# Two more groups per token pair with seven second products in layer 2, on paired operand sets

## The chip, the cores and the metric

One core of a Trainium2 chip runs the whole program. The metric is the device time of one execution in microseconds. An engine is TensorE (PE in the rows, PEld its weight loads), VectorE (DVE), ScalarE (ACT), GpSimd (POOL) or SyncE (SP).

## The reference

Attention over the channels (256) of 6016 tokens, then two feed-forward layers with 2048 hidden channels each. Only the second layer is changed:

```python
def _moe2_ref(x, w_in, w_out):      # x: 6016 x 256, w_in: 256 x 2048, w_out: 2048 x 256
    h = np.maximum(x @ w_in, 0.0)
    return (h * h @ w_out).astype(np.float32)
```

All of it is float32.

## The kernel before

Tokens are worked in six pairs of column blocks: five pairs of 2 x 512 tokens and one of 2 x 448. The hidden channels are worked in eight groups of 2 x 128. One pair and one group make a step; layer 1 takes steps 0 to 47, layer 2 steps 48 to 95. A 128 x 128 weight block times a block of tokens is a product. Both operands are split into a rounded high half and a low half, so a product is three matmuls: high by high, low by high, high by low. A split is a ScalarE copy (high half) and a VectorE subtraction (low half).

In a step the first products make a 2 x 2 block of hidden values (two rows of channels, two column blocks of tokens) out of a 2 x 2 block of weights and a 2 x 2 block of tokens. The Strassen-Winograd scheme does this with seven products in place of eight: p1 to p7, on sums of weights (made ahead) and sums of tokens (t1 to t4, made in `tokens`, line 770). The second products multiply the activated hidden block, 2 x 2, by a 2 x 2 block of output weights and add into PSUM over the eight groups. They are eight by the plain way and can be seven by the same scheme, if sums of hidden blocks are made in every step.

Layer 2's pairs 1 to 5 run through `first7s` (line 1583). Its PSUM banks X and Y hold the first products in turn. A bank is read out by ScalarE (`snap`) or added to by VectorE (`total`) before the next product may go on in it; Y also serves for those second products that have no bank of their own and are added to SBUF by VectorE (`flush`, line 1762). The four hidden blocks of a step lie in R[0] to R[3]: h11, h12, h21, h22. ReLU and square are two ScalarE operations (`relu`, `square`) or one VectorE operation (`both`).

`S2SET` (line 1459) names the groups with seven second products: 0, 2, 4, 6 of each pair, 0, 2, 4 of the last. For such a group three hidden blocks go straight into products (u[1], u[2], u[3], `items_direct`), and four sums (`tail`, line 1702) into four more (`items_sums`): t1 = R1 + R0 on VectorE, then t3 = R0 + R2, t2 = t1 + R2, t4 = R3 + t2 by three accumulating DMAs that GpSimd issues (`move`, line 1660). Each is split when it is made. The direct products stand in the next step, the four others three steps after the group's own. Other groups (plain) split all four blocks and have eight products in the next step (`items_plain`), two of which go through Y into `fz`. `finish_a` and `finish_b` (lines 1857, 1880) make the four output blocks of a pair in the first steps of the next, `finish_last` and `finish_rest` those of the last pair after all steps. `sums2` (line 1489) makes the sums of output weights for a group, once, ahead of pair 1.

The order of the work is computed ahead by the class `Plan` (line 28). TensorE and the DMA queue run in the order in which operations are added. For VectorE, ScalarE and GpSimd the planner simulates the engines with a fixed cost for each operation (`act_us`, `dve_us`, `MOVE_US`, `MOVE_LAT`) and issues each engine's operations by rank, which begins as the latest time at which each may start. `blame` looks for gaps of TensorE and lowers the rank of what they waited for; the best of 200 rounds is issued.

Of the kernel before, what the change touches and what calls it, by code (L numbers as in the profile page):

```python
# [18 lines left out]
P = 128  # L19
# [3 lines left out]
class Op:  # L23
    def __init__(self, eng, cost, lat, fn, deps):
        self.eng, self.cost, self.lat, self.fn, self.deps = eng, cost, lat, fn, deps


class Plan:
# [9 lines left out]
    ROUNDS = 200  # L38

    def __init__(self):  # L40
        self.ops = []
# [68 lines left out]
    def blame(self):  # L110

        for o in self.ops:
            if o.eng != "PE" or o.idle < 0.03:
                continue
            x = o
            while x.deps:
# [3 lines left out]
                x.rank -= 0.5 * min(1.0, o.idle + 0.2)  # L120

    def issue(self):
# [18 lines left out]
        for o in reversed(ops):  # L141
            for u in users[id(o)]:
                o.late = min(o.late, u.late - o.lat - o.cost)
            if o.eng == "DMA":

                o.late = queue = min(o.late, queue - o.cost)
        for o in ops:
            o.rank = o.late
        best = None
        for _ in range(self.ROUNDS):  # L150
# [3 lines left out]
            self.blame()  # L154
# [25 lines left out]
MOVE_US, MOVE_LAT = 0.9, 6.2  # L180
# [8 lines left out]
def tile_kernel(  # L189
# [50 lines left out]
    XS, GB, WB = 9, 4, 2  # L240
# [87 lines left out]
    def words(name, src, outs, lat=1.1):  # L328
# [3 lines left out]
        def f_e():  # L332
            t["e"] = cv_p.tile([P, 512], U32, tag="e", name="e")
            t["m"] = cv_p.tile([P, 512], U32, tag="m", name="m")
# [40 lines left out]
    def pair_of(name, src, place, *deps, lat=1.1):  # L375
# [5 lines left out]
        def f_e():  # L381
            t["e"] = cv_p.tile([P, 512], U32, tag="e", name="e")
            t["m"] = cv_p.tile([P, 512], U32, tag="m", name="m")
# [387 lines left out]
    def tokens(l, pr, parts=False):  # L771
# [28 lines left out]
        def tt(i):  # L800
            return t["t"][:, i, :n]

        def f_t3():
            t["t"] = xr_p.tile([P, 3, TB], F32, tag="t", name=f"xt{l}{pr}")
            V.tensor_tensor(tt(2), b(1, 1), b(0, 1), ALU.subtract)

        if plain(l, pr):
            todo = [(f"b{i + 1}{j + 1}", lambda i=i, j=j: b(i, j), load) for j in range(2) for i in range(2)]
            ts = []
        else:  # L810
            c = dve_us(n)
            sub = ALU.subtract
            t3 = ordered("xt", add("DVE", c, f_t3, load, xt_r.take()))
            t1 = add("DVE", c, lambda: V.tensor_tensor(tt(0), b(0, 1), b(0, 0), sub), t3)
            t2 = add("DVE", c, lambda: V.tensor_tensor(tt(1), b(1, 1), tt(0), sub), t1)
            t4 = add("DVE", c, lambda: V.tensor_tensor(b(0, 1), b(1, 0), tt(1), sub), t2)
            ts = [t1, t2, t3, t4]
            todo = [
# [1264 lines left out]
```

## Time and profile before

| what | before |
|---|---|
| device time, median of 3 runs | 1027.79 us (1026.01 to 1029.95) |
| the profiled execution | 1027.78 us |
| its span, first to last instruction | 1026.0 us |
| TensorE busy | 1019.3 us, 4565 matmuls |
| VectorE busy | 867.0 us, 1372 operations |
| ScalarE busy | 794.9 us, 1287 operations |
| GpSimd busy | 69.5 us, 78 operations |

Busy time is the union of an engine's instructions; consecutive ones overlap, so an instruction's printed length is more than its distance from the next. The first pair of layer 2 (plain second products) runs from about 550 to 628 us, pairs 1 to 4 from there to 941, the last to the end.

### The profile page before, as it was taken

To read this page: it belongs to the slowest core of one execution; us is meant where nothing else is said; L and a number is where in the kernel's file an instruction comes from. 1 tells how busy PE (TensorE), PEld (TensorE's weight loads), DVE (VectorE), ACT (ScalarE), POOL (GpSimd) and SP (SyncE) were. 2 spreads that over 40 slices of the span, in tenths; PEclk is the share of its full clock that TensorE was granted. 3 is DMA by queue.
4 is the path that set the end of the run, shared out by engine and by line. 5 is a ranking of instruction groups with operands and counts; after the bars stand their busy time and mean duration, and the time that the engine had idled before them with its cause. 6 is when DMAs were issued, how large, how long until landed. Compare 5 with 4: busy or idle time off the path is not lost.

```text
span 1026.0 us, 13020 instructions
## 1 busy us (share of the span) xinstructions
PE 1019.3 (99%) x4565; PEld 855.0 (83%) x4565; DVE 867.0 (85%) x1372; ACT 794.9 (77%) x1287; POOL 69.5 (7%) x78
## 2 busy tenths in 40 slices
PE   9999999999999999999999999999999999999998
PEld 7888888888888888888998888888888888888897
DVE  3999988888989899898778886788888888888876
ACT  5787667677778777768768978889889789789784
POOL 3400000000000000000000000111111111111110
PEclk9999999999999999999999999999999999999999
DMA  9657447435454644635745323655665665664661
GB/s 360 264 175 238 141 134 226 159 126 197 149 185 147 207 169 149 206 128 160 276 151 199 133 92 127 187 142 155 159 176 144 167 174 128 172 177 126 175 160 45
DMA packets 62609, 174.10 MB, mean 170 GB/s; under 512 B 6992, under 2 KB 10192, under 8 KB 61264
## 3 DMA queue, kind: packets, MB, share of 16 engines
q1 hardware_dynamic: 54336, 158.62, 46.0%
q0 software_dynamic: 8208, 14.65, 8.3%
q8 instruction: 36, 0.59, 0.2%
q14 instruction: 29, 0.24, 0.1%
HBM read 126.35 MB, written 32.24 MB: 155 GB/s over the span
## 4 chain that ended last, share of the span: by engine, by line
PE 97%; DMA 1%; DVE 0%; SPq 0%; ACT 0%; issue 0%
PE acc L1386 10%; PE acc L1392 10%; PE acc L1387 10%; PE xy L1602 6%; PE xy L1604 6%; PE xy L1603 6%; PE A L1293 4%; PE A L1294 4%; PE A L1295 4%; PE acc L1738 3%; PE acc L1740 3%; PE acc L1739 3%; PE s L925 3%; PE B L1295 2%; PE B L1293 2%; PE B L1294 2%
## 5 line engine op out<-in xcount | busy, mean ns | idle before, releaser
L1386 PE MATMUL acc<-g,wo 128*128 128x512 f32 (+1 forms) x448 | 172.9, 386 | 0.0
L1387 PE MATMUL acc<-g,wo 128*128 128x512 f32 (+1 forms) x448 | 172.9, 386 | 0.0
L1179 DVE TENSOR_TENSOR g<-r,g 128x1024 fp32r<-128x1024 f32 (+1 forms) x112 | 135.0, 1206 | 23.9 <-ACT g L1175 23.7
L1175 ACT ACTIVATE g<-r 128x1024 fp32r<-128x1024 f32 (+1 forms) x112 | 117.1, 1046 | 46.2 <-DVE r L1149 45.5
L1392 PE MATMUL acc<-g,wo 128*128 128x512 f32 (+1 forms) x448 | 136.6, 386 | 0.0
L1662 POOL DMA_DIRECT2D rs<-rs x57 | 49.3, 865 | 912.4 <-ACT rp L1633 601.5
L1652 DVE TENSOR_TENSOR gs<-rs,gs 128x512 fp32r<-128x512 f32 (+1 forms) x137 | 89.9, 674 | 14.6 <-ACT gs L1648 13.2
L1392 PEld LDWEIGHTS acc<-g,wo 128*128 128x128 f32 x448 | 84.1, 188 | 16.2
L1386 PEld LDWEIGHTS acc<-g,wo 128*128 128x128 f32 x448 | 84.1, 188 | 16.1
L1387 PEld LDWEIGHTS acc<-g,wo 128*128 128x128 f32 x448 | 84.1, 188 | 16.1
L1648 ACT ACTIVATE gs<-rs 128x512 fp32r<-128x512 f32 (+1 forms) x137 | 80.4, 613 | 6.1 <-DVE rs L1640 5.7
L1144 ACT ACTIVATE r<-hp,three 128x1024 f32<-128x1024 f32 (+1 forms) x40 | 45.3, 1132 | 49.0 <-DVE hp L1326 48.9
L1318 ACT ACTIVATE hp<-A 128x512 f32<-128x512 f32 (+1 forms) x96 | 56.6, 589 | 9.5 <-PE A L1295 8.6
L1602 PE MATMUL xy<-xt,w 128*128 128x512 f32 (+1 forms) x160 | 62.3, 389 | 0.0
L1604 PE MATMUL xy<-xt,w 128*128 128x512 f32 (+1 forms) x160 | 61.6, 385 | 0.0
L1603 PE MATMUL xy<-xt,w 128*128 128x512 f32 (+1 forms) x160 | 61.6, 385 | 0.0
L1149 DVE SCALAR_TENSOR_TENSOR r<-r,hp 128x1024 f32<-128x1024 f32 (+1 forms) x40 | 47.9, 1198 | 15.8 <-ACT r L1144 15.4
L1652 DVE TENSOR_TENSOR gs<-rp,gs 128x512 fp32r<-128x512 f32 (+1 forms) x80 | 52.4, 670 | 5.1 <-ACT gs L1648 5.1
L1738 PE MATMUL acc<-gs,wo 128*128 128x512 f32 (+1 forms) x141 | 54.2, 385 | 0.0
L1739 PE MATMUL acc<-gs,wo 128*128 128x512 f32 (+1 forms) x141 | 54.2, 384 | 0.0
L1740 PE MATMUL acc<-gs,wo 128*128 128x512 f32 (+1 forms) x141 | 54.2, 384 | 0.0
L1620 DVE TENSOR_TENSOR rp<-xy,rp 128x512 f32<-128x512 f32 (+1 forms) x60 | 40.5, 675 | 14.8 <-ACT rp L1614 10.2
(376 smaller groups left out, 2616.8 us busy)
## 6 DMA issues: line engine op xcount, KB each, us to landing
w<-w1d SPq DMA_DIRECT2D x176, 448.0 KB, 4.4
rs<-rs POOLq DMA_DIRECT2D x48, 256.0 KB, 3.3
qk<-in_qk_dram SPq DMA_DIRECT2D x8, 1024.0 KB, 16.3
w1d<-wA SPq DMA_DIRECT2D x16, 448.0 KB, 5.5
xr<-in_vT_dram SPq DMA_DIRECT2D x5, 1024.0 KB, 7.2
x2d<-o SPq DMA_DIRECT2D x20, 256.0 KB, 3.9
w1d<-wA SPq DMA_DIRECT2D x16, 256.0 KB, 2.6
w1d<-w SPq DMA_DIRECT2D x14, 256.0 KB, 2.7
```

The costliest lines, as they stand in the source:

```text
L1175: A.activation(t["g"][:, a:b, 0, :n], t["t"][:, a:b, :n], AF.Copy)
L1179: V.tensor_tensor(g[:, a:b, 1, :n], t["t"][:, a:b, :n], g[:, a:b, 0, :n].bitcast(F32), ALU.subtract)
L1386: T_.matmul(acc[b, e][:, :n], w(e, 0), gh_, start=first_of, stop=False)
L1387: T_.matmul(acc[b, e][:, :n], w(e, 1), gh_, start=False, stop=False)
L1392: T_.matmul(acc[b, e][:, :n], w(e, 0), gl_, start=False, stop=last_of_b)
L1602: T_.matmul(ps, wh, xh, start=start, stop=False, skip_group_check=True)
L1603: T_.matmul(ps, wl, xh, start=False, stop=False, skip_group_check=True)
L1604: T_.matmul(ps, wh, xl, start=False, stop=True, skip_group_check=True)
L1652: V.tensor_tensor(x[:, 1, :n], R[k].ap()[:, :n], x[:, 0, :n].bitcast(F32), ALU.subtract)
L1738: T_.matmul(ps, wh, gh, start=first, stop=False, skip_group_check=True)
L1739: T_.matmul(ps, wl, gh, start=False, stop=False, skip_group_check=True)
L1740: T_.matmul(ps, wh, gl, start=False, stop=last, skip_group_check=True)
```

## The change

Groups 0, 1, 3, 4, 5 and 7 of a pair have seven second products (0, 1, 3, 4 and 5 in the last). Their five products on hidden blocks and t1 stand in the next step, the three on t2, t3 and t4 three or four steps after the group's own (`S2AT`); a plain group's products stand partly in the next step, partly in the one after (`rest`). The hidden blocks lie in pairs: A2 holds R0 and R1, B2 holds R2 and R3, in four sets that take turns. R2 and R3 get one wide relu, one wide square and one wide split; t3 and t2 are made by one DMA that adds R2 to both and get one wide split; h11 is activated by VectorE alone. Operand tiles in layer 2 are halves of pairs as well. The space for them comes from the rings of layer 1 and the weight conversion. In `tokens` the sums t1, t2 and t4 overwrite the token blocks, and there are ten operand tiles in place of nine. The planner takes 150 rounds with drawn step sizes and doesn't blame gaps ahead of the step where the preparation of pair 1 starts. The diff, cut to its core:

```diff
 class Plan:
-    ROUNDS = 200
+    ROUNDS = 150
+    STEP = 0.25
+    SEED = 1
...
-    def blame(self):
+    def blame(self, rng):
         for o in self.ops:
-            if o.eng != "PE" or o.idle < 0.03:
+            if o.eng != "PE" or o.idle < 0.03 or o.n < self.settled:
                 continue
-            x = o
+            x, step = o, self.STEP * 2.0 * rng.rand()
...
-                x.rank -= 0.5 * min(1.0, o.idle + 0.2)
+                x.rank -= step * min(1.0, o.idle + 0.2)
...
-MOVE_US, MOVE_LAT = 0.9, 6.2
+MOVE_US, MOVE_LAT = 0.9, 5.6
...
-    XS, GB, WB = 9, 4, 2
+    XS, GB, WB = 10, 4, 2
...
+        t3 = ordered("xt", add("DVE", dve_us(n), f_t3, load, xt_r.take()))
+        t1 = less((0, 1), (0, 1), (0, 0), t3)
+        b11 = split_x("b11", lambda: b(0, 0), load)
+        b21 = split_x("b21", lambda: b(1, 0), load)
+        t2 = less((0, 0), (1, 1), (0, 1), t1, b11)
+        t4 = less((1, 0), (1, 0), (0, 0), t2, b21)
...
+        for k in (1, 0, 3, 2) if l and pr else range(4):
+            xt = split_x(*todo[k])
...
-    S2SET = {pr: (0, 2, 4, 6) if pr < NP - 1 else (0, 2, 4) for pr in range(1, NP)}
+    S2SET = {pr: (0, 1, 3, 4, 5, 7) if pr < NP - 1 else (0, 1, 3, 4, 5) for pr in range(1, NP)}
     S2ALL = sorted({g for gs in S2SET.values() for g in gs})
+    S2AT = {0: 3, 1: 5, 3: 6, 4: 7, 5: 9, 7: 10}
+    LAST_AT = {(NP - 1, 5): 8}
...
+        cells["R"] = [(rs[2 * k], rs[2 * k + 1]) for k in range(4)]
+        cells["fz"], cells["s1"] = rs[8].part
+        for name in ("d23", "t14", "p01", "t32"):
+            cells[name] = Duo(lambda: pools["g"].tile([P, 2, 2, TB], F32R, tag="g", name="gs"), g_r.take())
...
-        def move(k, j, *deps):
+        def move(dst, src, size, *deps):
             def f():
-                nc.gpsimd.dma_start(R[k].ap()[:, :n], R[j].ap()[:, :n], accum_op=ALU.add)
-            o = add("POOL", MOVE_US, f, *deps, lat=MOVE_LAT)
+                s = src.ap()[:, :n]
+                if size > 1:
+                    s = s.unsqueeze(1).to_broadcast([P, size, n])
+                nc.gpsimd.dma_start(dst.ap()[..., :n], s, accum_op=ALU.add)
+            o = add("POOL", MOVE_US + 0.3 * (size - 1), f, *deps, lat=MOVE_LAT + 1.7 * (size - 1))
...
             h11 = total(0, Y, p2, sn1)
-            g0 = square(0, relu(0, R[0], h11))
+            done[0] = both(0, h11)
...
             h21 = total(2, Y, p4, sn6)
-            g2 = square(2, relu(2, R[2], h21))
-            u[2] = split(2, names[2], g2)
+            r = act(AF.Relu, 0.08, B2, B2, 2, h22, h21)
+            done[2] = done[3] = act(AF.Square, 0, B2, B2, 2, r)
...
+        def splits():
+            x = split(B2, cells["d23"], 2, done[2])
+            u[2], u[3] = (part("d23", 0), *x), (part("d23", 1), *x)
+            if seven:
+                c = cells["d1"]
+                u[1] = (c, *split(R[1], c, 1, done[1]))
+            else:
+                for k in (0, 1):
+                    c = part("p01", k)
+                    u[k] = (c, *split(R[k], c, 1, done[k]))
+
+        def chain():
...
+            x = split(R[1], part("t14", 0), 1, t1)
+            u["t1"] = (part("t14", 0), *x)
+            u["move"] = done["t32"] = move(A2, R[2], 2, x, done[2])
+            done["t4"] = move(R[3], R[1], 1, done["t32"], u[3][1:])
+
+        def split_t():
+            x = split(A2, cells["t32"], 2, done["t32"])
+            u["t3"], u["t2"] = (part("t32", 0), *x), (part("t32", 1), *x)
+            c = part("t14", 1)
+            u["t4"] = (c, *split(R[3], c, 1, done["t4"]))
...
-        if -5 <= k < -1:
-            if k == -5:
+        if -6 <= k < 0:
+            if k == -6:
+                plan.settled = len(plan.ops)
                 extra_cells()
-            sums2(k + 5, S2ALL[k + 5])
+            sums2(k + 6, S2ALL[k + 6])
...
+            d, t = us.get(k - 1), us.get(due.get(k))
+            if d and d["seven"]:
+                d["chain"]()
+                d2, d3, d1, t5 = items_direct(d)
+                for i, x in zip((4, 5, 6, 6), (d2, d3, d1, t5)):
+                    gaps[i].append(x)
+            elif d:
+                x = items_plain(d)
+                gaps[4].append(x[1])
+                gaps[5].append(x[3])
+                gaps[6].extend([x[6], x[2], x[7]])
+                if (pr, g) == (NP - 1, NG - 1):
+                    gaps[6][:0] = [x[0], x[4], x[5]]
                 else:
+                    rest[k + 1] = x[0], x[4], x[5]
+            trio = rest.get(k) or (items_t(t) if t else None)
+            if trio:
+                for i, x in zip((0, 2), trio):
+                    gaps[i].append(x)
+                gaps[6].insert(-1, trio[2])
...
+            us[k]["splits"]()
+            if k + 1 in due:
+                us[due[k + 1]]["split_t"]()
             if k and g == 0:
                 finish_a(pr - 1)
-            if k >= NG and g == 1:
+            if k >= NG and g == 2:
                 finish_b(pr - 1)
...
     x = items_plain(us[max(us)])
+    t7, t6, t4 = items_t(us[due[max(us) + 1]])
+    t7()
+    t6()
     x[0]()
...
     x[5]()
+    t4()
     finish_rest(pr)
```

A gap is the place behind one of the seven first products, which come in the order p1, p2, p6, p7, p5, p4, p3.

## Rows read from the trace of the kernel before

**Rows 1.** The page: busy time, share and instructions of TensorE; clock by slice.

```profile
PE 1019.3 (99%) x4565; PEld 855.0 (83%) x4565; DVE 867.0 (85%) x1372; ACT 794.9 (77%) x1287; POOL 69.5 (7%) x78
...
PEclk9999999999999999999999999999999999999999
```

**Rows 2.** Waits of TensorE, whole span: total us, times, longest us.

```profile
PE warm L953 <- DVE ebias L866: 1.1, 1, 1.1
...
PE s L925 <- DMA qk<-in_qk_dram: 0.7, 1, 0.7
```

**Rows 3.** Windows, one pair: busy us (count) of PE, PEld, DVE, ACT, POOL; clock, DMA.

```profile
704.40:783.30 78.90, 78.90 (x348) 64.92 (x348) 67.13 (x109) 67.68 (x125) 10.34 (x12) 1.00 0.60 159
```

**Rows 4.** Timeline of TensorE: start us, length us, line, operation.

```profile
782.68 0.39 PE L1740 MATMUL xy<-gs,w2x 128*128 128x512 f32 x1
...
785.40 0.39 PE L1604 MATMUL xy<-xb,w 128*128 128x512 f32 x1
...
960.39 0.36 PE L1602 MATMUL xy<-xb,w 128*128 128x448 f32 x1
...
963.03 0.36 PE L1739 MATMUL acc<-gs,wo 128*128 128x448 f32 x1
```

**Rows 5.** Timeline, narrow operations in a row; then groups by line, 680 to 1000 us.

```profile
713.84 1.66 ACT L1648 ACTIVATE gs<-rs 128x512 fp32r<-128x512 f32 x3
...
715.46 1.89 DVE L1652 TENSOR_TENSOR gs<-rs,gs 128x512 fp32r<-128x512 f32 x3
...
L1648 ACT ACTIVATE gs<-rs 128x512 fp32r<-128x512 f32 x96 | 57.2, 623 | 4.2 <-DVE rs L1640 4.0
...
L1652 DVE TENSOR_TENSOR gs<-rs,gs 128x512 fp32r<-128x512 f32 x96 | 64.3, 686 | 11.0 <-ACT gs L1648 10.1
```

**Rows 6.** Single lines, wide operations of other stages: ns min/median/max, first and last start.

```profile
L1179 DVE TENSOR_TENSOR g<-r,g x98: 1084/1226/1228, 101.3 to 596.8; 128x1024 fp32r<-128x1024 f32 x82, 128x896 fp32r<-128x896 f32 x16
...
L1175 ACT ACTIVATE g<-r x99: 945/1062/1071, 100.0 to 599.2; 128x1024 fp32r<-128x1024 f32 x83, 128x896 fp32r<-128x896 f32 x16
```

**Rows 7.** Windows of layer 1 and of layer 2's first pair, columns as in rows 3.

```profile
60.00:140.00 80.00, 80.00 (x354) 66.24 (x354) 78.53 (x138) 56.95 (x91) 0.00 (x0) 1.00 0.57 181
...
300.00:480.00 180.00, 180.00 (x798) 149.33 (x797) 164.28 (x246) 136.42 (x191) 0.00 (x0) 1.00 0.49 164
...
580.00:590.00 10.00, 10.00 (x46) 8.29 (x45) 9.86 (x19) 8.93 (x14) 0.00 (x0) 1.00 0.25 86
```

**Rows 8.** Timeline, a snap behind the last matmul of its product.

```profile
706.95 0.39 PE L1604 MATMUL xy<-xt,w 128*128 128x512 f32 x1
...
707.37 0.60 ACT L1614 ACTIVATE rs<-xy 128x512 f32<-128x512 f32 x1 [0.40 <-PE xy L1604]
```

**Rows 9.** Line 1602, first matmul of a first product: what it waited for, 640 to 1013 us.

```profile
  DVE rp L1620: 1.6, 8
```

**Rows 10.** Line 1662, the moves, whole span; then the DMA queues, 680 to 1000 us.

```profile
L1662 POOL DMA_DIRECT2D rs<-rs x57: 862/862/1010, 641.9 to 1001.2; - x57
...
DMA to landing us min/median/max: 3.1/3.3/6.8
...
q0 software_dynamic: 7166, 12.82, 23.3%
```

**Rows 11.** Line 573, the weight loads of the first products, 640 to 1000 us.

```profile
DMA to landing us min/median/max: 3.1/4.4/6.9
```

**Rows 12.** Timeline of the tail: TensorE and VectorE.

```profile
1013.84 0.62 DVE L1773 TENSOR_TENSOR f<-xy,f 128x448 f32<-128x448 f32 x1 [0.17 <-PE xy L1740]
...
1014.05 0.37 PE L1740 MATMUL acc<-gs,wo 128*128 128x448 f32 x1
1014.52 0.47 PE L1738 MATMUL xy<-gs,wo 128*128 128x448 f32 x1
...
1021.85 0.37 PE L1740 MATMUL acc<-gs,wo 128*128 128x448 f32 x1
1022.25 0.62 DVE L1852 TENSOR_TENSOR c<-acc,c 128x448 f32<-128x448 f32 x1
```

More of the change, by code (lines that the diff above doesn't have):

```diff
@@ L798, in b, with split_x, f_hi, f_lo @@
             return t["r"][:, i, j * n : (j + 1) * n]
-        def tt(i):
-            return t["t"][:, i, :n]
         def f_t3():
[L804 to L818, printed above, removed]
-                ("b11", lambda: b(0, 0), load), ("b21", lambda: b(1, 0), load), ("t3", lambda: tt(2), t3),
-                ("t2", lambda: tt(1), t2), ("t4", lambda: b(0, 1), t4), ("t1", lambda: tt(0), t1),
-                ("b22", lambda: b(1, 1), load),
-            ]
-        for name, src, ready in todo:
+            t["t"] = xr_p.tile([P, TB], F32, tag="t", name=f"xt{l}{pr}")
+            V.tensor_tensor(t["t"][:, :n], b(1, 1), b(0, 1), ALU.subtract)
+        def split_x(name, src, ready):
             p = {}
-            def f_hi(p=p, name=name, src=src):
+            def f_hi():
                 p["x"] = x_p.tile([P, 2, TB], F32R, tag="x", name=f"x{name}")
                 A.activation(p["x"][:, 0, :n], src(), AF.Copy)
-            def f_lo(p=p, src=src):
+            def f_lo():
                 V.tensor_tensor(p["x"][:, 1, :n], src(), p["x"][:, 0, :n].bitcast(F32), ALU.subtract)
@@ new lines, in extra_cells, with __init__, take, use @@
+        deps = all_of(wA_r)
+        for k in range(2, 6):
+            cells["x", k] = Cell(lambda: wA.tile([P, 2, 4, P], F32R, tag="wA", name="w2x"), deps)
+    class Duo:
+        def __init__(self, make, deps):
+            whole = Cell(make)
+            self.ap, self.home = whole.ap, self
+            self.part = [Cell(part_of(whole, k), deps) for k in range(2)]
+            for c in self.part:
+                c.home = self
+        def take(self):
+            return [c.take() for c in self.part]
+        def use(self, *ops):
+            for c in self.part:
+                c.use(*ops)
@@ L1587, in first7s @@
         seven = by7(l, pr, g)
-        even = g % 2 == 0
-        sets = cells["R", even]
-        R = sets[g // 2 % len(sets)]
-        names = ("d0", "d1", "d2", "d3") if even else ("p0", "p1", "p2", "p3")
+        A2, B2 = cells["R"][g % 4]
+        R = A2.part + B2.part
         X, Y = cells["X"], cells["Y"]
@@ L1675, in steps @@
             Y.use(h11)
-            g0 = square(0, relu(0, R[0], h11))
-            if not seven:
-                u[0] = split(0, names[0], g0)
+            done[0] = both(0, h11)
             yield
@@ L1686, in steps @@
             p5 = product(X, False, "s1", "t1", sn6)
+            u["p5"] = p5
             h22 = total(3, X, p5, sn7)
-            g3 = both(3, h22)
-            u[3] = split(3, names[3], g3)
             yield
@@ L1693, in steps @@
             Y.use(h21)
-            g2 = square(2, relu(2, R[2], h21))
-            u[2] = split(2, names[2], g2)
+            r = act(AF.Relu, 0.08, B2, B2, 2, h22, h21)
+            done[2] = done[3] = act(AF.Square, 0, B2, B2, 2, r)
             yield
             p3 = product(X, False, "s4", "b22", h22)
-            r = relu(1, X, p3, R[1].take())
+            r = act(AF.Relu, 0.08, R[1], X, 1, p3, R[1].take())
             X.use(r)
-            g1 = square(1, r)
-            u[1] = split(1, names[1], g1)
```

208 lines of the change are left out of this document (98 added, 110 removed).

## The prediction

> **What bounds the kernel now.** I read the page's busy line first, then who TensorE waits for, then windows of the stage that is changed, then single operations. TensorE is busy 99% of the span at a granted clock of 1.00 (the 2.4 GHz level) throughout [rows 1]. All of its waits that the trace names lie in the opening, 0.7 to 1.1 us each [rows 2]. In a whole token pair of layer 2 it is busy 78.90 of 78.90 us for 348 matmuls, while VectorE is busy 85% and ScalarE 86% of it [rows 3]. So in this stage a matmul that is taken away shortens the run by what a matmul takes, provided that the other engines still deliver on time. What a matmul takes is its distance from the next and not the 0.39 us printed beside it, since they overlap: from 782.68 to 785.40 stand 12 matmuls of 512 columns, 0.2267 us each, and from 960.39 to 963.03 13 of 448 columns, 0.2031 us each [rows 4]. The pair agrees: 348 x 0.2267 = 78.89 us. A product is three matmuls, 0.68 us; I call that a slot.
>
> **Products removed.** A group with seven second products has one product less. By the sets in the diff, pairs 1 to 4 go from four such groups to six (8 more), the last pair from three to five (2 more). That is 8 x 3 x 0.2267 = 5.44 us and 2 x 3 x 0.2031 = 1.22 us, together 6.66 us, all on the path while TensorE has no idle time. A step now holds 14 products (15 where the group before it is a plain one), a pair 6 x 14 + 2 x 15 = 114 in place of 116: 77.5 us.
>
> **Work on VectorE and ScalarE.** I count operations from the code. Per pair before, VectorE has 13 in a group of seven products, 9 in a plain one and 20 at the turn of the pair (7 low halves, 4 sums, 9 outputs): 4 x 13 + 4 x 9 + 20 = 108, the row has 109. ScalarE has 4 x 16 + 4 x 13 + 8 = 124, the row 125 [rows 3]. After, VectorE has 9 narrow and 2 wide operations in a group of seven, 7 and 1 in a plain one: 88 narrow, 14 wide a pair. ScalarE has 8 narrow and 4 wide, 7 and 3: with its 8, 70 narrow and 30 wide. Three narrow ones in a row take 1.89 us on VectorE, the last alone 0.69, so one costs 0.60; on ScalarE 1.66 and 0.62, so 0.52 [rows 5]. Wide ones of the same kinds stand in other stages: 1.23 us on VectorE, 1.06 on ScalarE [rows 6]; I take these as they stand, which is the upper end, since they overlap like the narrow ones (1.14 and 0.96 by the same 0.09 and 0.10 us would be the lower). VectorE: 88 x 0.60 + 14 x 1.23 = 70.0 us (68.8 at the lower end). ScalarE: 70 x 0.52 + 30 x 1.06 = 68.2 us (65.2). Of 77.5 us that is 89 to 90% and 84 to 88%. On the same count the pair before is 108 x 0.60 = 64.8 (82%) and 124 x 0.52 = 64.5 (82%): ScalarE's load grows little, VectorE's by 4 to 5 us a pair. That is dense, but TensorE runs without a gap beside a VectorE that is busy 98% (60 to 140 us) and 91% (300 to 480 us) [rows 7], with the same wide operations in the latter. I cost it at nothing; if the cover were gone, each pair could lose at most what VectorE is late, and it has 7.5 us to spare.
>
> **Deadlines inside a step.** A step's order becomes p1, a t product, p2, p6, a t product, p7, p5, direct, p4, direct, p3, direct, t4, t5. A snap starts 0.19 us after the slot of its product ends (slot of the matmul at 706.95 ends at 707.18, ScalarE starts at 707.37) and takes 0.60 [rows 8]; two slots, 1.36 us, lie between p1 and p6, so 0.57 us is left. A total on VectorE (0.69) has 0.48 us left, and so has the flush of t5, which had a third slot ahead of the next p2 (t5, t4, p1, t7) and now has two. These gaps are as narrow today for the snaps and totals, and the trace shows how narrow: 8 times in 370 us the weight load of such a product waited for a total, 0.2 us each, without a gap in the matmuls as long [rows 9]. The paired split is later: total, wide relu, wide square, wide high half, wide low half are 0.19 + 0.69 + 3 x 1.06 + 1.23 = 5.3 us from the end of p4, against 3.5 us in narrow ones, and the first direct product is due 12 slots (8.2 us) later; 2.9 us stay. What is next late is t1: from the end of p3 seven operations, about 4.7 us, before t5, 16 slots (10.9 us) on. It came two steps later before. I cost all of this at nothing as the order of each engine is written by a planner that knows these sizes; the price where it fails is the first rival.
>
> **Moves.** Three DMAs per group become two, one of them double; 19 x 3 = 57 become 29 x 2 = 58. A narrow one occupies GpSimd for 0.86 us and lands in 3.1 to 6.8 us, median 3.3 [rows 10]. Fifty of them in 320 us took 23.3% of the engines' time, 1.49 us each. The double one is not in the trace: issue between 0.86 and 1.72 us, landing between 3.3 us (as the narrow median) and 8.3 (maximum plus 1.49); I take 3.3 + 1.5 = 4.8, nearest to the median row. The chain t1, its split, double move, last move counted in slots from the start of the group's own step: t1 is split by 11 + (2.7 + 2.0) / 0.68 = 18, the double move lands by 27 (33 at the long end), the last one by 33 (44), and with their splits t2 and t3 are ready by 30 to 36, t4 by 35 to 46. The first is due at slot 43 at the earliest, t4 at 54. Nothing on the path. GpSimd's queue holds nothing else here. DMA share goes from 0.60 [rows 3] to (0.60 x 78.9 + 6 x 1.49) / 77.5 = 0.73. The weight loads land in 3.1 to 6.9 us [rows 11], and have a step, 9.5 us: still covered.
>
> **The rest.** The token operands are now made in place: t2 may be written only after b11 is split, t4 after b21. That puts a high and a low half (0.62 + 0.69 us, rows 5) ahead of t2 at 11 pair starts; a tenth operand tile lets one more of them be made before the old pair ends. Bounds: 0 to 11 x 1.31 = 14.4 us, below nothing excluded since TensorE waits for none of these today [rows 2]. I take 0. Two more sums of output weights stand in steps before the first pair; VectorE is at 99% there for one stretch [rows 7], but they are spread over six steps in place of four, 0. The planner's 200 rounds become 150 with drawn step sizes, and gaps of TensorE ahead of that point no longer change ranks; the code of layer 1 stays, its order may not.
>
> **The tail.** Before, TensorE stood from 1014.26 to 1014.52 for a flush that ended at 1014.46 [rows 12]. In the new tail three products stand between, so 0.26 us goes. The last product ended at 1022.22, and the last VectorE operation began at 1022.25 [rows 12]; t4 becomes the last product, and that operation again follows it at once. No change.
>
> **Sum.** 6.66 + 0.26 = 6.9 us off the profiled execution, span 1026.0 and 1027.78 us in all (1.8 around it), which is also the median of the runs (1027.79). Forecast 1020.9 us, 0.67% less. About 0.5%, 5.1 us, is what a measurement of this kernel can tell from no change: below 1022.7 counts as faster.
>
> **Rivals.** First, a wide operation in front of a snap or total. ScalarE would be inside a wide one 30 x 1.06 / 77.5 = 41% of the time and VectorE 14 x 1.23 / 77.5 = 22%. Met at a random point, a wide one delays by more than the spare 0.57 us by (1.06 - 0.57)^2 / 2.12 = 0.11 us on average on ScalarE and (1.23 - 0.48)^2 / 2.46 = 0.23 us on VectorE. With 24 snaps and 16 totals or flushes of two slots a pair: 24 x 0.41 x 0.11 + 16 x 0.22 x 0.23 = 1.9 us a pair, 9.5 us over five pairs. An order blind to it gives 1020.9 + 9.5 = 1030.4, slower than before; from 6.9 us on the change loses, that is 0.17 us in each of 40 steps. An order that avoids three of four gives 1023.3. Against it: the waits today sum to almost nothing with the same spare times [rows 9]. For it: the narrow 0.62 us hardly exceeds the spare 0.57, the wide one does.
> The Trainium skill has the rule for this side, page "Perfetto Trace Analysis", section "Optimizing Scalar/DVE Operations": grouping into larger operations helps where the engine is saturated, and where Scalar or Vector aren't saturated but cause bubbles on others, breaking instructions up may let work finish sooner. By that rule, with both engines at 85%, the result is this rival.
>
> Second, layer 1 loses order: VectorE at 91 to 98% there has little to give, and the later t2 adds to it. At a third of the bound above, 14.4 / 3 = 4.8 us, 1025.7; at all of it 1035.
>
> Third, the moves come late because the DMA engines are fuller: if each of the 29 double moves made TensorE wait the 1.49 us it is longer, 43 us, 1064. It needs the spare 7 to 13 slots to be gone, for which nothing in the trace speaks.
>
> Fourth, the change does not remove the products: excluded but for a slip, 1028.
>
> **How the numbers follow.** Forecast 0.57 (1019.3 to 1022.6, the lower end by the 0.15% by which runs fall below the median); first rival in part 0.18 (1022.6 to 1028), in full 0.10 (1028 to 1040); layer 1 0.09 (most of it 1023 to 1031); late moves 0.04; no removal 0.02. Faster: 0.57 and a little of the partial cases, 0.60. Slower by over 5 us (above 1032.9): half of the full first rival, a third of layer 1, the moves, 0.12. Same: the rest, 0.28. The range reaches over the partial cases: 1019.3 to 1027.5.
>
> **What would show it.** Right: 30 matmuls fewer (4535), TensorE without waits from 60 us on, pairs of 77.5 us, VectorE busy near 90% in them. Wrong for the first rival: waits of matmuls for snaps, totals or the flush behind 1.06 to 1.23 us operations. Wrong for layer 1: pair times before 560 us longer. Wrong for the moves: the splits of t2, t3 or t4 released by a DMA, and TensorE by them. A span that ends more than 4.2 us after the last matmul starts would break the last step.

## The result and the profile after

The changed kernel takes **1036.64 us** (median, 1033.47 to 1039.02) beside 1028.29 us (1026.01 to 1029.95) of the kernel before: a ratio of 1.0077, 95% interval [1.0052, 1.0101]. It is slower by 0.8%, where 1020.9 us was forecast and the range ended at 1027.5. The profiled execution took 1038.69 us, with a span of 1036.8; it lies 2 us above the median.

First the page of the changed kernel, to be held against [rows 1]: busy time and instructions of each engine, and the shares of the chain of work that ended last.

```profile
span 1036.8 us, 12887 instructions
...
PE 1019.8 (98%) x4535; PEld 846.5 (82%) x4535; DVE 890.2 (86%) x1355; ACT 790.5 (76%) x1170; POOL 81.4 (8%) x79
...
PEclk9999999999999999999999999999999999999999
...
PE 55%; DMA 21%; issue 18%; DVE 2%; ACT 2%; POOL 1%; SPq 0%; DVEq 0%; POOLq 0%; ACTq 0%
```

The 30 matmuls are gone (4565 to 4535) and the clock is what it was, yet TensorE's busy time is not shorter. A late matmul hides part of its own delay: the one before it is shown for 0.39 us, though the next normally follows after 0.2267, and the late one is itself shown for 0.50 (the last line of the example below). The chain says more: 21% of it is DMA, in a kernel whose TensorE had bounded it from end to end [rows 1, 2]. That share says where to look and not what it costs: plain_source below has the same 21% and is 4 us faster.

Next the waits, from 640 us to the end: of TensorE, then those of ScalarE that a DMA ended (waiter, releaser, total us, times, longest us). Before, neither engine had a wait for a DMA in this stretch, and TensorE had no wait at all [rows 2].

```profile
PE xy L1618 <- ACT rc L1630: 2.2, 4, 0.8
PE xy L1767 <- DVE rc L1636: 1.9, 1, 1.9
PE xy L1618 <- ACT rp L1650: 1.8, 1, 1.8
...
ACT gs L1656 <- DMA rc<-rc: 10.6, 8, 2.8
ACT gs L1656 <- DMA rs<-rs: 9.4, 9, 2.2
```

Then windows of one pair each, roughly, columns as in [rows 3]:

```profile
704.00:783.00 79.00, 78.24 (x341) 63.32 (x340) 69.91 (x101) 65.86 (x100) 12.61 (x12) 1.00 0.76 180
783.00:862.00 79.00, 77.67 (x336) 62.08 (x334) 68.99 (x100) 64.05 (x96) 12.63 (x12) 1.00 0.75 179
862.00:941.00 79.00, 76.73 (x332) 61.68 (x333) 68.61 (x101) 64.70 (x99) 12.66 (x12) 1.00 0.70 174
```

A pair now holds 342 matmuls by the sets, and 79 us don't suffice for them: 341, 336, 332 fit in. None of the other engines is full. VectorE is busy 87 to 88%, ScalarE 81 to 83%, much as worked out ahead, and the DMA engines 70 to 76% (forecast 73%).

**Where the 10.8 us of span lie.** They are those of the two profiled executions; the medians lie 8.4 us apart. I cut both spans at the first matmul of the paired groups and at the start of the last matmul. The opening with layer 1: 627.78 us before, 628.36 after, +0.6. The paired groups: 394.07 and 402.67, +8.6. The end behind the last matmul: 4.15 and 5.73, +1.6. In the middle part I add up how far the distance between two matmuls exceeds its normal value (0.2267 us for 512 columns, 0.2031 for 448; [rows 4]), where it does so by 0.05 us or more: 1.3 us before, 15.8 after. So 394.07 - 6.66 for the removed matmuls + 14.5 = 401.9, which is the measured 402.67 but for 0.8. I call this sum **late time** below; it is what every experiment is read by.

**One place as an example.** This timeline of the changed kernel has the columns start us, length us, engine, line, operation, and in brackets what ended the wait before it:

```profile
915.21 1.22 POOL L1677 DMA_DIRECT2D rc<-rc  x1 [10.34 <-DVE rs L1636]
...
922.34 0.63 ACT L1656 ACTIVATE gs<-rs 128x512 fp32r<-128x512 f32 x1
...
925.76 1.06 ACT L1656 ACTIVATE gs<-rc 128x1024 fp32r<-128x1024 f32 x1 [2.79 <-DMA rc<-rc]
...
926.03 0.91 POOL L1677 DMA_DIRECT2D rc<-rc  x1 [9.61 <-DMA rc<-rc]
...
926.72 1.04 ACT L1650 ACTIVATE rp<-rp 128x1024 f32<-128x1024 f32 x1
...
927.67 0.58 ACT L1650 ACTIVATE rp<-xy 128x512 f32<-128x512 f32 x1
...
928.30 0.50 PE L1618 MATMUL xy<-xb,w 128*128 128x512 f32 x1 [1.77 <-ACT rp L1650]
```

The double move is issued at 915.21 and lands 10.5 us later. ScalarE has come to the high half of t2 and t3, which needs that DMA, and stands for 2.79 us. It works in order: the relu of another group (926.72, 927.67) is queued behind, and the product that needs the buffer it frees starts 1.93 us later than the cadence. The late DMA never shows up as a wait of TensorE. It shows as a wait for ScalarE, by way of an operation that had nothing to do with the DMA.

### The profile page after: what moved, and what is told of

It reads as the page before. It is cut to its first block, busy times and chain, and to the rows that moved or that the text cites. A ratio compares the mean times of both kernels' runs of the same rounds, so it can differ in the third digit from the quotient of the medians.

```text
span 1036.8 us, 12887 instructions
## 1 busy us (share of the span) xinstructions
PE 1019.8 (98%) x4535; PEld 846.5 (82%) x4535; DVE 890.2 (86%) x1355; ACT 790.5 (76%) x1170; POOL 81.4 (8%) x79
## 3 DMA queue, kind: packets, MB, share of 16 engines
q0 software_dynamic: 12064, 22.32, 12.1%
## 4 chain that ended last, share of the span: by engine, by line
PE 55%; DMA 21%; issue 18%; DVE 2%; ACT 2%; POOL 1%; SPq 0%; DVEq 0%; POOLq 0%; ACTq 0%
PE acc L1400 8%; PE acc L1399 8%; PE acc L1405 8%; DMA rc<-rc 6%; DMA rs<-rs 6%; DMA rp<-rp 5%; PE A L1306 3%; PE A L1307 3%; PE A L1308 3%; DMA qk<-in_qk_dram 3%; PE B L1306 2%; PE B L1307 2%; PE B L1308 2%; PE xy L1618 1%; PE xy L1620 1%
## 5 line engine op out<-in xcount | busy, mean ns | idle before, releaser
L1405 PEld LDWEIGHTS acc<-g,wo 128*128 128x128 f32 x448 | 84.1, 188 | 16.1
L1399 PEld LDWEIGHTS acc<-g,wo 128*128 128x128 f32 x448 | 84.1, 188 | 16.1
L1400 PEld LDWEIGHTS acc<-g,wo 128*128 128x128 f32 x448 | 84.1, 188 | 16.1
L1677 POOL DMA_DIRECT2D rs<-rs x20 | 22.5, 1126 | 695.2 <-DVE gs L1661 631.3
L1162 DVE SCALAR_TENSOR_TENSOR r<-r,hp 128x1024 f32<-128x1024 f32 (+1 forms) x40 | 47.9, 1198 | 13.7 <-ACT r L1157 13.3
L1661 DVE TENSOR_TENSOR gs<-rc,gs 128x512 fp32r<-128x512 f32 (+3 forms) x48 | 42.2, 882 | 13.5 <-ACT gs L1656 13.4
L1656 ACT ACTIVATE gs<-rs 128x512 fp32r<-128x512 f32 (+3 forms) x50 | 38.9, 786 | 17.1 <-DMA rs<-rs 9.4
L1618 PE MATMUL xy<-xb,w 128*128 128x512 f32 (+1 forms) x120 | 48.2, 402 | 3.2 <-ACT rp L1650 1.8
L1767 PE MATMUL acc<-gs,wo 128*128 128x512 f32 (+1 forms) x131 | 50.6, 387 | 0.0
L1769 PE MATMUL acc<-gs,wo 128*128 128x512 f32 (+1 forms) x131 | 50.6, 386 | 0.0
L1768 PE MATMUL acc<-gs,wo 128*128 128x512 f32 (+1 forms) x131 | 50.4, 384 | 0.0
L1339 DVE TENSOR_TENSOR hp<-B,hp 128x512 f32<-128x512 f32 (+1 forms) x48 | 32.6, 680 | 19.6 <-PE B L1308 15.2
```

Of the source, the lines that this page charges most:

```text
L1399: T_.matmul(acc[b, e][:, :n], w(e, 0), gh_, start=first_of, stop=False)
L1400: T_.matmul(acc[b, e][:, :n], w(e, 1), gh_, start=False, stop=False)
L1405: T_.matmul(acc[b, e][:, :n], w(e, 0), gl_, start=False, stop=last_of_b)
L1618: T_.matmul(ps, wh, xh, start=start, stop=False, skip_group_check=True)
```

## Experiments

**Theory.** The double move takes far longer than the 4.8 us I gave it, the order was made for 8.5 us (1.2 of issue and 7.3 behind it), and so the splits behind it, ScalarE behind the splits, and TensorE behind ScalarE are late. **Rivals:** wide operations stand in front of short ones (the prediction's first rival); the order was found by a poorer search; the repeated source makes the double move slow; any order with so little spare time is late.

All runs in one table; each time stands beside that of the kernel before on the same chip, as a ratio with its 95% interval. "Groups" is the middle part of the span, "late" its late time, "end" the part behind the start of the last matmul, and "DMA waits" what ScalarE waited for DMAs from 640 us on. These four are of the profiled execution, the median is of all.

| kernel | median us | ratio | groups us | late us | end us | DMA waits us |
|---|---|---|---|---|---|---|
| before | 1028.29 | 1 | 394.07 | 1.3 | 4.1 | 0 |
| after | 1036.64 | 1.0077 [1.0052, 1.0101] | 402.67 | 15.8 | 5.7 | 20.0 |
| no_moves | 1025.28 | 0.9960 [0.9948, 0.9972] | 389.64 | 3.0 | 5.7 | 0 |
| two_moves | 1026.49 | 0.9980 [0.9970, 0.9991] | 391.66 | 5.3 | 5.7 | 4.1 |
| plain_source | 1032.67 | 1.0042 [1.0026, 1.0057] | 396.54 | 10.0 | 5.7 | 10.4 |
| lat8 | 1045.75 | 1.0158 [1.0136, 1.0181] | 408.16 | 21.5 | 6.0 | 22.9 |
| gpsimd_adds | 1049.20 | 1.0208 [1.0194, 1.0222] | 414.06 | 26.3 | 5.1 | 0 |
| two_moves_5us | 1036.94 | 1.0099 [1.0069, 1.0128] | 400.29 | 13.6 | 5.4 | 15.9 |
| two_moves_queue | 1033.94 | 1.0065 [1.0045, 1.0084] | 397.99 | 10.5 | 5.3 | 16.1 |
| old_search | 1034.37 | 1.0063 [1.0046, 1.0080] | 400.13 | 13.2 | 5.7 | 19.4 |
| before_lat34 | 1057.38 | 1.0290 [1.0275, 1.0306] | 422.48 | 29.6 | 4.2 | 33.8 |
| three_moves_7us | 1024.42 | 0.9964 [0.9951, 0.9976] | 389.86 | 3.7 | 5.9 | 7.3 |
| three_moves_seed1 | 1028.09 | 1.0000 [0.9989, 1.0011] | 392.93 | 5.3 | 5.7 | 6.9 |
| after_seed2 | 1039.02 | 1.0107 [1.0087, 1.0127] | 406.24 | 19.2 | 5.9 | 23.1 |

The last column goes with the late time: up to 7.3 us of waiting the late time is 1.3 to 5.3 us, from 15.9 on it is 10.5 to 29.6. gpsimd_adds is the exception and has another reason.

### no_moves: the moves left out, order and splits kept

```diff
-                nc.gpsimd.dma_start(dst.ap()[..., :n], s, accum_op=ALU.add)
+                dst.ap(), src.ap()
```

> The two accumulating DMAs of each group are left out (t2, t3 and t4 are then split without R2 or t2 added, so the products on them are on other numbers); the order of TensorE, VectorE and ScalarE is that of the changed kernel, operation by operation. Theory A (ScalarE and VectorE, which run in order, stand behind a split whose double move lands later than the planner reckoned, and snaps and relus behind it come late to TensorE): the waits go, 1036.6 falls by the 14.5 us that the gaps between matmuls are above their normal distance, to about 1022. Theory B (wide operations of 1.05 to 1.22 us in front of snaps and totals): nothing of this kind changes, 1034 to 1037. In between, 1026 to 1031, both have a share.

Measured: 1025.28 us, 11.4 us less than the changed kernel, and 12.8 us of its 15.8 us of late time are gone. From 640 us on TensorE has no wait that the trace names. A window of this kernel, columns as in [rows 3]:

```profile
704.00:783.00 79.00, 79.00 (x348) 64.87 (x348) 71.34 (x104) 67.53 (x103) 0.00 (x0) 1.00 0.37 125
```

TensorE is busy without a gap while VectorE is at 90% and ScalarE at 85%, with every wide operation in place. So the moves cost the time, and the wide operations at most 3.0 - 1.3 = 1.7 us in five pairs. The 1025.28 us, 3 us above the time expected, is also what this order can reach at best; it stays above 1020.9 by the 1.6 us at the end, these 1.7 us, and what is within the runs' spread.

### two_moves: the double move as two narrow ones, one behind the other

```diff
-                nc.gpsimd.dma_start(dst.ap()[..., :n], s, accum_op=ALU.add)
+                for k in range(size):
+                    nc.gpsimd.dma_start(dst.part[k].ap()[:, :n], s, accum_op=ALU.add)
```

> The double move (512 KB, source read twice) becomes two narrow DMAs of 256 KB from the same sources into the same halves, issued one behind the other; all else as in the changed kernel. Theory A, if the size of one transfer is what makes it late: narrow ones landed in 3.3 us before, two of them about 5 us behind the first issue, in place of 8.8; the waits go, 1022 to 1025. If the bytes are what counts and not the transfer: landing stays at 8 to 9 us, 1034 to 1038. Theory B: no change, 1034 to 1038.

Measured: 1026.49 us; 10.2 us come back by this edit alone, with the planner's figures untouched. Issues with KB each and median us from issue to landing, 640 to 1020 us, first of the changed kernel, then of this one:

```profile
rs<-rs POOLq DMA_DIRECT2D x8, 512.0 KB, 8.8
rp<-rp POOLq DMA_DIRECT2D x8, 512.0 KB, 8.9
rc<-rc POOLq DMA_DIRECT2D x8, 512.0 KB, 8.0
```

```profile
rs<-rs POOLq DMA_DIRECT2D x24, 256.0 KB, 5.1
rp<-rp POOLq DMA_DIRECT2D x24, 256.0 KB, 6.7
rc<-rc POOLq DMA_DIRECT2D x24, 256.0 KB, 3.8
```

The second list looks as if the bytes landed sooner in two pieces, but it mixes both pieces with the group's third move. From the first issue until both pieces have landed it is 8.6 us in the median of the 29 groups, beside 8.8 for the double move, and 11.7 at most, beside 12.1. What has changed is the start. The first piece waits only for the addition that makes t1 and not for t1's split: it is issued 0.5 us behind that addition in the median, the double move 2.1 us behind it. Both sums are complete 9.4 us behind it in place of 10.8, and the third move lands after 13.3 in place of 16.7. So the time of theory A came true without its reason (about 5 us of landing): what this run shows is what an earlier start is worth, and not that smaller transfers land sooner.

### plain_source: the double move reads two different tiles side by side

```diff
-                s = src.ap()[:, :n]
-                if size > 1:
-                    s = s.unsqueeze(1).to_broadcast([P, size, n])
+                s = other.ap()[..., :n]
```

> The double move reads R2 and R3, side by side, in place of R2 twice (the sum for t2 is then on another block); same size, same place. If the source that is read twice makes the double move slow: landing falls from 8.8 us towards 4.8, time to 1022 to 1026. If it is the size: landing 8 to 9 us, time 1033 to 1039.

It adds other data; the bytes are the same, 22.3 MB in the queue of the moves, in 8992 packets in place of 12041. The issue falls from 1.20 us in the median (up to 1.58) to 0.86 (up to 1.48), and the landing to 8.6, 8.7 and 7.7 us. That gives 4.0 us back, of the 11.4 that no_moves gave, and lies just below the time expected if the size were all. So the repeated source has a part. How the rest divides between the size and the start behind t1's split these runs don't show; both sums are complete 10.2 us behind t1's addition here, between two_moves and the changed kernel, and so is the late time.

### lat8: the double move's figure behind its issue raised from 7.3 to 8.0 us

```diff
-            o = add("POOL", MOVE_US + 0.3 * (size - 1), f, *deps, lat=MOVE_LAT + 1.7 * (size - 1))
+            o = add("POOL", MOVE_US + 0.3 * (size - 1), f, *deps, lat=MOVE_LAT if size == 1 else 8.0)
```

> Only the planner's figure for the double move is changed: landing 8.0 us behind the end of its issue, as the trace of the changed kernel has it in the median, in place of 7.3. Theory A in its plain form (a wrong figure, and the order can be mended): 1022 to 1027. Theory A in the stronger form (the double move is too long for the places at which its sums are due, whatever the order): TensorE waits for the splits instead of for snaps, 1028 to 1036. Theory B: 1034 to 1039.

This missed: a truer figure made it 1045.75 us. The new order puts narrow moves of another group right behind double ones, for which it still reckons 5.6 us behind the issue. Timeline of this kernel:

```profile
682.23 1.20 POOL L1677 DMA_DIRECT2D rs<-rs  x1 [7.16 <-DVE gs L1661]
...
682.96 1.39 POOL L1677 DMA_DIRECT2D rc<-rc  x1
...
691.40 0.63 ACT L1656 ACTIVATE gs<-rc 128x512 fp32r<-128x512 f32 x1 [2.35 <-DMA rc<-rc]
...
692.57 0.50 PE L1618 MATMUL xy<-xt,w 128*128 128x512 f32 x1 [1.60 <-ACT hs L1630]
```

The narrow move of 682.96 lands 8.4 us after its issue, where the median of all narrow ones before was 3.3 [rows 10]; the double one, issued 0.7 us ahead of it, has landed 1.8 us earlier. These two land one behind the other, and no single figure for a move holds that.

### gpsimd_adds: GpSimd adds, no DMA

```diff
-                nc.gpsimd.dma_start(dst.ap()[..., :n], s, accum_op=ALU.add)
+                nc.gpsimd.tensor_tensor(d, d, s, ALU.add)
-            o = add("POOL", MOVE_US + 0.3 * (size - 1), f, *deps, lat=MOVE_LAT + 1.7 * (size - 1))
+            o = add("POOL", pool_us(size * n), f, *deps)
```

> The accumulating DMAs become additions by GpSimd itself (one of 128 x 1024 with R2 read twice, one of 128 x 512 per group); the planner gets 0.15 + 0.0022 us per column for them and no landing time. Theory A: what hurt was the landing; without it TensorE has no waits, 1022 to 1026 as with the moves left out. Rival: GpSimd's additions and VectorE's get in each other's way (VectorE is busy 87% of this stage), operations of VectorE grow beyond 0.69 us and the gain is lost again: above 1030.

The worst of the variants of the changed kernel, for another reason. Groups by line, 680 to 1000 us (total us, mean ns), first two of the changed kernel, then the same of this one, which are the two that grew most of their shapes:

```profile
L1661 DVE TENSOR_TENSOR gs<-rs,gs 128x1024 fp32r<-128x1024 f32 x14 | 17.1, 1218 | 1.4 <-ACT gs L1656 1.4
...
L1661 DVE TENSOR_TENSOR gs<-hs,gs 128x512 fp32r<-128x512 f32 x14 | 9.6, 683 | 0.0
```

```profile
L1678 POOL TENSOR_TENSOR rp<-rp 128x1024 f32<-128x1024 f32 x7 | 21.8, 3119 | 46.1 <-DVE gs L1661 46.1
...
L1661 DVE TENSOR_TENSOR gs<-rs,gs 128x1024 fp32r<-128x1024 f32 x13 | 19.0, 1460 | 0.0
...
L1661 DVE TENSOR_TENSOR gs<-hs,gs 128x512 fp32r<-128x512 f32 x14 | 13.8, 988 | 0.0
```

These means hide that few operations grow, and by much. From 630 us on 38 of 501 VectorE operations are over 15% longer than the median of their kind in the changed kernel, where none is; the longest takes 2.89 in place of 0.68 us. The medians of the splits stay: 679 beside 683 ns for 128x512, 1214 beside 1217 for 128x1024. In all VectorE's operations take 41 us more, and TensorE's waits are now for VectorE (8.4 us for f, 6.7 us for a total). The rival came true. The Trainium skill, page "GPSIMD Engine Reference", section "Key points", has it that GpSimd shares its memory interfaces with VectorE and contends with VectorE operations of two inputs there; this run agrees.

### two_moves_5us and two_moves_queue: two narrow moves with other figures

```diff
-            o = add("POOL", MOVE_US + 0.3 * (size - 1), f, *deps, lat=MOVE_LAT + 1.7 * (size - 1))
+            o = add("POOL", MOVE_US if size == 1 else 1.8, f, *deps, lat=4.5 if size == 1 else 5.0)
```

> Two narrow moves in place of the double one, and the planner reckons 1.8 us of issue and 5.0 us of landing for both, 4.5 us for the third, in place of 1.2 and 7.3, 5.6. Two narrow moves alone gave 1026.5 under the old figures. If their figures were too long and the order gave room away for that: 1022 to 1025, below the kernel before. If the shorter figure takes the room that the real landing (5 to 7 us) needs: 1026 to 1032.

```diff
+            o = add("POOL", 3.4 if size > 1 else 1.7, f, *deps, lat=3.4 if size > 1 else 3.0)
```

> Two narrow moves, and the planner holds GpSimd for as long as the transfers take in one queue (3.4 us for the two, 1.7 us for the third) and adds 3.4 and 3.0 us of landing, since in the last runs a move that was issued right behind another landed late. Theory: the order now knows that moves wait for each other; 1021.5 to 1024.5. If moves don't wait for each other and landing is set by the other transfers: like the run beside it, 1024 to 1029.

Measured: 1036.94 and 1033.94 us, 10 and 7 us above two_moves, although the DMAs are the same ones. The moves are issued and complete at the same place in TensorE's order, within 3 matmuls in the median. With the shorter figures the planner puts the splits that need them earlier: ScalarE reaches some of its wide splits up to 24 matmuls sooner, and waits 15.9 and 16.1 us for DMAs in place of 4.1; late time is 13.6 and 10.5 us in place of 5.3. Both missed the times expected, and pointed to what a figure is for: it has to cover the late landings, not the typical one.

### old_search: the planner's search as before

```diff
-    ROUNDS = 150
+    ROUNDS = 200
```

The fixed step of 0.5 and the treatment of early gaps are restored too.

> The changed kernel with the planner's search as it was: 200 rounds, a fixed step of 0.5, no bound on the gaps that are blamed. If the search is a part of the loss (an order made for its own figures that leaves no room): 1028 to 1032. If any order on the double move loses, because the sums are due too soon for it: 1034 to 1042.

1034.37 us with 13.2 us of late time: the search is not the cause.

### before_lat34: the kernel before with the median landing as its figure

```diff
-MOVE_US, MOVE_LAT = 0.9, 6.2
+MOVE_US, MOVE_LAT = 0.9, 3.4
```

> The kernel before with the planner's figure for a move's landing at 3.4 us (the median landing that its trace shows) in place of 6.2 us. Theory (the figure is what leaves a move its margin, since its landing scatters from 3 to 7 us and it queues behind the one before it): the moves come nearer to their due steps, the operations of ScalarE and VectorE behind them wait for some, and the kernel is slower than before by 2 to 10 us (0.2 to 1 %). Rival (the kernel before has so much idle time that the figure doesn't matter): within 1 us of before, with stage gaps near 1.3 us. Rival (a truer figure lets the planner order better): faster by 1 to 3 us.

The clearest of all: the kernel before, with not one operation changed, becomes 29 us slower, 1057.38 us. That is more than I expected (2 to 10). Its waits from 640 us on, then the landing of its moves, and one place:

```profile
PE xy L1602 <- ACT rp L1614: 20.6, 15, 2.1
...
ACT gs L1648 <- DMA rs<-rs: 33.8, 17, 3.7
```

```profile
DMA to landing us min/median/max: 3.1/3.4/7.9
```

```profile
931.05 0.86 POOL L1662 DMA_DIRECT2D rs<-rs  x1 [3.11 <-DMA rs<-rs]
...
938.59 0.63 ACT L1648 ACTIVATE gs<-rs 128x512 fp32r<-128x512 f32 x1 [3.73 <-DMA rs<-rs]
...
939.12 0.58 ACT L1614 ACTIVATE rp<-xy 128x512 f32<-128x512 f32 x1
...
939.76 0.50 PE L1602 MATMUL xy<-xt,w 128*128 128x512 f32 x1 [2.13 <-ACT rp L1614]
```

It is the picture of the changed kernel, nearly once for each of the 19 groups of seven, and with narrow moves alone. What the planner allows from issue to landing can be held against each landing in the trace:

| kernel and moves | allowed us | landings: median, maximum us | later than allowed | by, in sum us |
|---|---|---|---|---|
| before | 0.9 + 6.2 = 7.1 | 3.3, 6.8 | 0 of 57 | 0 |
| before_lat34 | 0.9 + 3.4 = 4.3 | 3.4, 7.9 | 21 of 57 | 47.0 |
| after, double | 1.2 + 7.3 = 8.5 | 8.8, 12.1 | 17 of 29 | 15.1 |
| after, third | 0.9 + 5.6 = 6.5 | 4.0, 9.0 | 11 of 29 | 10.2 |
| lat8, double | 1.2 + 8.0 = 9.2 | 8.3, 10.8 | 5 of 29 | 5.1 |
| lat8, third | 0.9 + 5.6 = 6.5 | 5.3, 11.7 | 9 of 29 | 20.0 |
| three_moves_7us | 0.9 + 7.0 = 7.9 | 6.1, 10.0 | 18 of 87 | 14.0 |

In the kernel before no move landed later than its figure allowed. Taking that away makes it as late, with its three narrow moves, as the changed kernel is and more. A landing beyond its figure is not a loss by itself, though: three_moves_7us, the next experiment, has 18 of them and only 3.7 us of late time. The sums tell more than the counts: 0, 14.0, 25.3 (after), 25.1 (lat8) and 47.0 us of lateness stand beside 1.3, 3.7, 15.8, 21.5 and 29.6 us of late time.

### three_moves_7us, three_moves_seed1, after_seed2: three separate moves, and two orders of each kernel

```diff
-            u["move"] = done["t32"] = move(A2, R[2], 2, x, done[2])
-            done["t4"] = move(R[3], R[1], 1, done["t32"], u[3][1:])
+            t2 = move(R[1], R[2], 7, x, done[2])
+            done["t32"] = [t3, t2]
+            done["t4"] = move(R[3], R[1], 7, t2, u[3][1:])
```

Ahead of t1's split stands `t3 = move(R[0], R[2], 7, t1, done[2])`; the third argument is now the landing figure, and the random seed is 2.

> The changed kernel with its three moves of a seven-product group as three narrow ones, each planned by itself: t3 waits only for its own addition, t2 for the split of t1, and each is reckoned with 7.0 us behind 0.9 us of issue (the planner's random seed is another, too). Theory (the double move lands late in what the planner leaves it, and ScalarE and TensorE stand behind it): the first narrow move starts 1 to 3 us earlier, each lands in 6 to 8 us, so the stage has matmul distances above normal of 3 to 6 us as with two narrow moves in a row (5.3), and the time is 1022 to 1027 us, faster than the kernel before by 0.1 to 0.6 %. Rival (an order with less work and no spare time is late whatever the moves are): gaps of 10 us or more, 1032 us or more. Rival (the wide operations cost): no nearer to the kernel without moves (1025.3) than the changed kernel.

> The three narrow moves with 7.0 us each, with the random seed of the changed kernel: another order of the same operations. Theory (the moves' size and the margin in the figure give the time back, not a lucky order): 1022 to 1028 us, within 3 us of the three moves with the other seed (1024.4), matmul distances above normal in the stage of 3 to 7 us. Rival (the other seed's order did it): 1030 us or more, gaps of 10 us or more, as in the changed kernel.

> The changed kernel, double moves and all figures as they are, with the random seed of the faster three-move kernel: another order of the same operations. Theory (double moves that land late in what the planner leaves them): 1033 to 1042 us, gaps in the stage of 11 to 20 us, whatever the seed. Rival (the changed kernel's loss is that of one unlucky order): 1028 us or less, gaps of 6 us or less.

The three moves give 1024.42 us with one seed and 1028.09 with the other; the double move 1039.02 and 1036.64. So the order drawn is worth 2 to 4 us, and the moves 8.5 us with the one seed and 14.6 with the other: not a lucky order. Size, start and figure of the moves are changed together here, and are not told apart. three_moves_7us is **faster than both kernels**, by 0.36% [0.24, 0.49] than the one before. With the other seed it is level with the one before, and 3.7 us from the first where I expected at most 3: whether the change gains anything depends on the order drawn, too. The waits of TensorE that are left in three_moves_7us from 640 us on:

```profile
PE xy L1618 <- ACT rs L1650: 0.7, 1, 0.7
PE xy L1766 <- DVE hs L1636: 0.5, 1, 0.5
PE xy L1618 <- ACT rp L1630: 0.2, 1, 0.2
PE xy L1618 <- ACT rc L1630: 0.2, 1, 0.2
```

## Why the prediction was wrong, point by point

- **Products removed: right.** 30 matmuls are gone, and where nothing is late that is worth what was said: no_moves has 389.64 us of groups, and 394.07 - 6.66 with 1.7 us more of late time makes 389.1.
- **Work on VectorE and ScalarE: right.** Estimated 70.0 and 68.2 us a pair; nearly without late time the window of no_moves has 71.3 and 67.5 in 79 us, which is 70.0 and 66.2 in the 77.5 us of the estimate.
- **Deadlines in a step (first rival): nearly at nothing.** 1.7 us in the five pairs, close to the 2.4 us of its partial case, far from the 9.5 us in full. The rule cited there from the Trainium skill's page "Perfetto Trace Analysis", section "Optimizing Scalar/DVE Operations", had spoken against this change; here the measurement decides, for in no_moves the trace names no wait of TensorE behind a wide operation.
- **Moves: this step failed, in two numbers.** The landing was sized at 4.8 us, near the narrow median, with 8.3 as the long end; the median of the 29 is 8.8 us, the longest 12.1. And the spare 7 to 13 slots weren't there. I counted from the earliest time at which t1 can be split, slot 18. In the example above the group's step begins at 896.36 and its double move is issued at 915.21: slot 28 (18.85 / 0.68). Its landing at 925.76 is slot 43, which is just where I had the first of its products due. What lies between slots 18 and 28 is other groups' operations, which VectorE and ScalarE issued ahead of this chain: t1's split ends only at 914.46. The planner had no reason to hurry the chain, since its ranks begin as the latest starts that the figures allow, and those allowed 8.5 us, which 17 of the 29 exceeded. The "nothing" that I gave the moves was 12.8 us.
- **The third rival** had the late moves, but 43 us as their price and 0.04 as its chance. Its sign came true by half: a DMA released the splits, but TensorE waited for relus and snaps behind them (4.9 us), and hardly for the splits (0.2 us). "For which nothing in the trace speaks" was wrong: the diff gives the figures, [rows 10] gave a maximum of 6.8 us for half the bytes, and a wait that is absent today says nothing of how much was to spare.
- **Layer 1: right.** In the two windows of layer 1 in [rows 7] TensorE has no gap and VectorE is as busy as before within 0.2 us; the 0.6 us ahead of the groups lie in the opening, and within its spread: that part takes 625.4 to 630.6 us in the 14 profiled executions.
- **Tail: wrong by 1.6 us.** The 0.26 us ahead of the last flush are gone, within the difference of the late times: behind 1003 us no distance is 0.05 us above normal. The end of the changed kernel, to be held against [rows 12]:

```profile
1031.03 0.36 PE L1769 MATMUL acc<-gs,wo 128*128 128x448 f32 x1
...
1031.21 0.61 DVE L1877 TENSOR_TENSOR f<-B,f 128x448 f32<-128x448 f32 x1
...
1031.74 0.61 DVE L1877 TENSOR_TENSOR rc<-acc,rc 128x448 f32<-128x448 f32 x1
...
1032.27 0.61 DVE L1877 TENSOR_TENSOR c<-acc,c 128x448 f32<-128x448 f32 x1
...
1033.26 0.40 SPq L1854 DMA_DIRECT2D out_dram<-c  x1
```

The last operation of VectorE begins 1.24 us after the last matmul in place of 0.40, since two other outputs stand before it, and SP then issues it last of four. I had looked at which product comes last, and not at how many sums fall due with it.

The sum, made again with what was measured: 6.66 us off, 14.5 us of late time on (12.8 of them the moves'), 1.6 at the end, 0.6 in the opening and 0.8 unassigned: +10.8 us of span.

**What stays open.** A figure of 8.0 us for the double move came out 9 us above one of 7.3. The table shows where: the double moves were late by 5.1 us in sum in place of 15.1, the third ones, whose figure stayed, by 20.0 in place of 10.2. A figure that depends on the queue wasn't tried with double moves. And how much of a landing is the other transfers' share: their traffic stands beside each long landing looked at, but no run took the weight loads away.

## What to carry to other kernels

Where a planner writes the order, an operation's latency figure is also the margin it leaves: give it the late end of the landings, with the queue that the order will make, and not the median (7.9 us under a longest landing of 10.0 did in three_moves_7us; 4.3 under 7.9 did not in before_lat34), and ask of every new or larger transfer whether its figure lies above what it will take, before counting spare slots in a chain that the planner is free to start late. A transfer whose sources are ready at different times is better left in pieces, each waiting for its own source. And a late DMA is to be looked for behind the engine that works in order: TensorE's waits named ScalarE, and only ScalarE's waits named the DMA.

## What the runs showed of the hardware

- An accumulating move of 256 KB lands 3.1 us after its issue at best and 3.3 in the median [rows 10], one of 512 KB in the changed kernel 4.7 at best and 8.8 in the median, 12.1 at most. Two windows of the changed kernel, each from the issue of a double move to its landing, with no other move under way but the end of a narrow one in the first 0.8 us of the second (columns as in [rows 3]):

```profile
715.30:721.40 6.10, 6.10 (x28) 5.06 (x27) 5.44 (x9) 5.60 (x9) 1.16 (x1) 1.00 1.03 274
724.20:733.10 8.90, 8.90 (x41) 7.38 (x40) 7.90 (x12) 7.27 (x11) 1.20 (x1) 1.00 0.82 197
```

  The DMA engines are full in the first and busy 82% in the second. The moves' queue has 47.0% of the first window and 35.7% of the second, 2.9 and 3.2 us of all engines' time, about twice the 1.49 us of a narrow one. The rest is other traffic: two weight loads of 448 KB and a store of 256 KB in the first, two weight loads and a load of 256 KB in the second. So a mean share of 0.73 hides stretches in which a large move has to share full engines. The fit in the Trainium skill's page "DMA: Bandwidth & Descriptors", section "Anatomy of one DMA — SWDGE (gpsimd) path", gives 2.6 and 3.2 us as an estimate for these sizes; the measurement decides.
- A repeated source makes the issue on GpSimd longer: 1.20 us in the median, beside 0.86 for a plain source of the same size.
- GpSimd's additions of 128x1024 take 2.8 us in the median (2.4 to 3.9). Beside them few VectorE operations are longer, 38 of 501, but some by as much as a whole such addition: 0.68 to 2.89 us.
